# Moving the feed-forward part, the normalised rows and the next rows' flip within the two-layer steps of an interleaved attention and feed-forward kernel

## The chip, the cores and the metric

The kernel runs on one core of a Trainium2 chip. The metric is the device time of one execution in microseconds (us). Three runs of the kernel before the change took 1553.95, 1558.8 and 1562.65 us; their median is 1558.8 us.

The engines of a core work in parallel, each in the order of its own instructions: TensorE (PE in the profile; its weight loads are PEld), VectorE (DVE), ScalarE (ACT), GpSimd (POOL) and SyncE (SP, which here only issues DMAs). They wait for each other through semaphores. TensorE writes to PSUM, which has eight banks.

## The reference

Two layers, each of a recurrent attention part A and a gated feed-forward part B, over 2048 rows of 448 columns:

```
x = x + A(layernorm(x));  x = x + B(layernorm(x))     # layer 1
x = x + A(layernorm(x));  return x + B(layernorm(x))  # layer 2, the same weights

A: for each of 64 segments of 32 rows:
     h = [mem (8 rows), segment (32 rows)]
     q, k, v = h Wq, h Wk, h Wv        # 16 heads of 256
     o = softmax(mask(q k^T / 16)) v, through Wo
     mem = o[:8];  output o[8:]
B: ((max(x Wg, 0)) * (x Wu)) Wd        # 448 -> 1792 -> 448
```

A segment needs the memory that the segment before it leaves, so A is a chain of 64 steps in each layer.

## The kernel before, in words

**Chains and steps.** Layer 1 and layer 2 run as two chains, the second four segments (`LAG`) behind the first. Step `g` does segment `g` of the first chain and segment `g - 4` of the second in the same matmuls, 2 x 40 moving columns. There are 68 steps; `active(g)` says which chains are live, and `two` is true where both are. Every second step (odd `g` from 3 on) also carries the feed-forward part (`Feed`, called `ff`) of 128 rows: 64 of layer 1 and 64 of layer 2. These are the long steps; 30 of them have both chains, and the change touches these alone ("two-layer long steps").

**Before the steps** the weights are folded: `A_sb` holds Wq Wk^T by heads, `B_sb` Wv Wo. So a step has these matmuls:

- `project` (L714): 28 tiles of h with `A_sb` into PSUM tiles `prj`, in banks of six or four tiles (the order is `BANKS`). Half 0 is heads 0 to 7, half 1 the rest. `copies` takes each bank to `TQ` or `TZ`, on DVE or ACT. Of the four chunks of 128 columns, the last holds 64 columns only; `project_early` (L699) does that chunk for four banks ahead of the others, as the first thing of a step, and holds their banks.
- `scores` (L840): `Sm` against the memory and `Sx` against the segment's own rows, each with a softmax on DVE and ACT whose parts (`m0`, `m1`, `x0`, `x1`, index 0 to 3) the step calls one by one.
- `weigh_m`, `weigh_x`: probabilities times h (`ya`, `yb`, `y1`, `y2`), copied to `YB` (Y in the profile). `weigh_x` of a step runs at the start of the next.
- `project_out` (L932): `YB` times `B_sb` into `ox`, 28 tiles (`NT`) of three matmuls for each half; `project_last` (L940) does the last 64 columns into `o3` (o in the profile).
- `finish`: `ox` to the next step's memory columns in `hT` and to `OT`, the rows that A leaves, transposed.

**The feed-forward part of a long step:**

- `residual` (L556): four transposes of `OT` (`otp`), the sum with the rows `xa` on DVE, then `row_stats`: two statistics on DVE and two operations on POOL that make 1/sqrt(variance).
- `norm` (L583): the normalised rows `xn`, on DVE. `fetch` (L586) writes `xn` to DRAM (`dxn`) and reads it back transposed into `xT`, two DMAs issued by SP, the second when the first has landed.
- `open_rows` (L595): opens six PSUM banks (`ups`, `gps`) with the 64-column chunk; it is the first reader of `xT`. `products` and `gated` do the rest, `down` (L652) multiplies with Wd into `dps`, adds and takes statistics; `norm2` (L672) normalises layer 1's rows for layer 2 (`xn` again).
- `feed_on` (L678): four transposes of that `xn` (`tps`) and two copies into the next steps' `hT`: one on DVE, one on ACT.

**What sets the order.** TensorE's order is that of the code: `in_order` ties every matmul to the one before it. `InOrder` does the same for DVE, ACT and SP. Which PSUM bank a tile gets is chosen while the program is built: `bank` (L130) keeps an estimate of when each bank is free, counted in estimated ns of matmul time, and takes the earliest that nothing holds; `after` is the estimated time from the last matmul to the end of the copies. A wrong estimate makes no wrong result: the matmul waits for the copy.

Of the kernel before, what the change touches and what calls it, by code (L numbers as in the profile page):

```python
# [9 lines left out]
F32 = mybir.dt.float32  # L10
# [18 lines left out]
BLK = 2  # L29
TB = BLK * SEG  # L30
NT = 28
# [10 lines left out]
BANKS = (((0, 6), (6, 6), (24, 4), (12, 6), (18, 6)), ((0, 6), (24, 4), (6, 6), (12, 6), (18, 6)))  # L42
# [8 lines left out]
def a_tile(t):  # L51

    if t >= 24:
        return t
    u = t // 12 * 6 + t % 6
    return 3 * (t // 6 % 2 * 4 + u % 4) + u // 4
# [7 lines left out]
def build_kernel(ctx, tc, A_x, A_mem0, A_Wq, A_Wk, A_Wv, A_Wo, B_W_gate, B_W_up, B_W_down, out,  # L64
                 ntiles=16, nseg=64):
    nc = tc.nc
    P = nc.NUM_PARTITIONS
# [62 lines left out]
    def bank(shape, dtype, name, after=700, hold=False):  # L130

        i = min((i for i in range(8) if i not in held), key=lambda i: free_at[i])
        t = psum.tile(shape, dtype, tag=f"b{i}", name=name)
        bank_of[t.name] = (i, after)
        free_at[i] = now[0] + 1000
        if hold:
            held.add(i)
        return t
# [39 lines left out]
    pre = prepare.enter_context(tc.tile_pool(name="pre", bufs=6))  # L178
# [69 lines left out]
    def next_piece():  # L248

        if pieces:  # L250
            spread(sp.dma_start(*pieces.pop(0)))

    hTb = []
# [61 lines left out]
    with prepare:  # L315
# [130 lines left out]
        for p in range(NP):  # L446
            hf, p4 = divmod(p, 4)
# [37 lines left out]
        for p in range(NP):  # L485
            hf, p4 = divmod(p, 4)
# [205 lines left out]
    def tile_of(ps, hf, t, i, chains, hb, j, kds, first, last):  # L692

        n = L * len(chains)
        for kd in kds:
            mm(ps[:, i * n:(i + 1) * n], A_sb[:, kd, hf, a_tile(t), :], moving(hb, j, kd, chains),
               start=first and kd == kds[0], stop=last and kd == kds[-1], skip_group_check=True)

    def project_early(hf, chains, hb, j, pairs=(0, 1), head=0):  # L699

        n = L * len(chains)
        pre = {}
        for pair in [EARLY[i] for i in pairs]:
            for i0 in pair:
                pre[i0] = bank([P, 512], F32, "prj", hold=True)
            for i in range(head):
                tile_of(pre[pair[0]], hf, pair[0] + i, i, chains, hb, j, range(3), i == 0, False)
            for i in range(6):
                for i0, rows in zip(pair, (slice(0, 64), slice(64, 128))):
                    mm(pre[i0][:, i * n:(i + 1) * n], A_sb[rows, 3, hf, a_tile(i0 + i), :], moving(hb, j, 3, chains, rows),  # L710
                       start=(i == 0 and (head == 0 or i0 != pair[0])), stop=False, skip_group_check=True)
        return pre

    def project(hf, chains, hb, j, banks, pre={}, busy=False, first=None, inside=None, head=0):  # L714

        n = L * len(chains)
        for i0, k in banks:
            ps = pre[i0] if i0 in pre else bank([P, 512], F32, "prj")
            two = len(chains) == 2

            def copies(eng, rows, T):
                if two:
                    evac(eng, T, ps[rows, 0:k * n].rearrange("p (t g q) -> p t g q", t=k, q=16))
                    return
                c = chains[0]
                src = ps[rows, 0:k * n].rearrange("p (t w) -> p t w", t=k)
                x, m = (0, SEG) if c == 0 else (MEM, 0)
                evac(eng, T[:, :, 2, MEM * c:MEM * c + MEM], src[:, :, m:m + MEM])
                evac(eng, T[:, :, 3 * c:3 * c + 2, :],
                     src[:, :, x:x + SEG].rearrange("p t (g q) -> p t g q", q=16))  # L730

            for i in range(k):
                if inside is not None and i == 4:
                    inside()
                if i0 not in pre:
                    tile_of(ps, hf, i0 + i, i, chains, hb, j, range(4), True, True)
                elif i >= head or i0 != banks[0][0]:
                    tile_of(ps, hf, i0 + i, i, chains, hb, j, range(3), False, True)
            if i0 in pre:
                let_go(ps)  # L740
            if first is not None:
                first()
            if i0 < 24:
                u0, eo = i0 // 12 * 6, i0 // 6 % 2
                T = TQ[hf][:].rearrange("p g u w -> p g (u w)").rearrange("p g (t e q) -> p t e g q", e=2, q=16)
                T = T[:, u0:u0 + 6, eo]
                copies(act if (i0 != 6 if busy and hf else i0 % 12) else dve, slice(0, P), T)
            else:
                for eng, e in ((act if busy else dve, 0), (act, 1)):
                    copies(eng, FR[e], TZ[hf][FR[e]].rearrange("p g (t e q) -> p t e g q", e=2, q=16)[:, :, e])  # L750
            if i0 in (6, 18):
                next_piece()
# [58 lines left out]
    def step(g, ff, pre, late):  # L811
        chains = active(g)
        xs = active(g - 1)
        ms = [c for c in chains if g - c * LAG + 1 < nseg]
        gb, j = divmod(g, BLK)
        hb = hTb[gb % 2]
# [115 lines left out]
        def project_out(hf, t0, t1):  # L932

            for t in range(t0, t1):
                for mc in range(3):
                    mm(ox[:, mc, lo:hi], B_sb[:, hf, t, mc * 128:(mc + 1) * 128],
                       YB[hf][:, t, lo:hi], start=(hf == 0 and t == 0 and mc == 0),
                       stop=(hf == 1 and t == NT - 1 and mc == 2), skip_group_check=True)
# [39 lines left out]
                    ff.gate_up(u)  # L978


        project(0, chains, hb, j, BANKS[0][0:2], pre)
        hk = hk_make()
        if ff is not None:
            ff.residual()
        next_piece()
        project(0, chains, hb, j, BANKS[0][2:5], pre, ff is not None)
        two = len(chains) == 2
        if ff is not None:
            ff.norm()
            if two:  # L990
# [11 lines left out]
        between = len(chains) == len(xs) == 1  # L1002
# [56 lines left out]
        if ff is not None:  # L1059
            x1[3]()  # L1060
            if len(chains) == 1:
                x0[0]()
                x1[0]()
            ox_open()
            project_out(0, 0, 10)
            ff.open_rows((0, 1, 2))
            if len(chains) == 2:
                x0[0]()
            x0[1]()
            m1[2]()  # L1070
            x0[2]()
            if two:
                px0 = fetched(PX[0], "x0")
            feed(0)
            next_piece()
            if len(chains) == 2:
                x1[0]()
            ff.products(1)
            ff.gated(1)
            pm = flipped(PM[1], 1, "m1", act) if ms else None  # L1080
            x1[1]()
            ff.products(2)
            x1[2]()
            if two:
                px1 = fetched(PX[1], "x1")
            else:
                px0 = flipped(PX[0], 2, "x0", act)
            weigh_m(1, hk, pm)
            ff.gated(2)
            feed(3)  # L1090
            project_out(0, 10, 18)
            next_piece()
            ff.down()
            ff.norm2()
            project_out(0, 18, NT)
            project_last()
            next_piece()
            project_out(1, 0, 12)
            if not two:
                px1 = flipped(PX[1], 2, "x1")  # L1100
            project_out(1, 12, 18)
            ff.feed_on()
            project_out(1, 18, NT)
        else:
            next_piece()
            ox_open()
            m1[2]()
            x0[0]()
            x0[1]()
            late_flip = 23  # L1110
            project_out(0, 0, late_flip)
            pm = flipped(PM[1], 1, "m1") if ms else None
            project_out(0, late_flip, NT)
            weigh_m(1, hk, pm)
            x0[2]()
            x1[3]()
            x1[0]()
            x1[1]()
            x1[2]()
            if two:  # L1120
                px1 = fetched(PX[1], "x1")
            next_piece()
            project_last()
            project_out(1, 0, 10)
            px0 = flipped(PX[0], 2, "x0", act)
            project_out(1, 10, 25)
            if not two:
                px1 = flipped(PX[1], 2, "x1", act)
            next_piece()
            project_out(1, 25, NT)  # L1130
        finish()
        nxt = active(g + 1)
        pre = project_early(0, nxt, hTb[(g + 1) // BLK % 2], (g + 1) % BLK) if nxt else {}
        weigh_x(0, hk, px0)
        return pre, lambda between: weigh_x(1, hk, px1, between)

# [3 lines left out]
    pre, late = project_early(0, active(0), hTb[0], 0), None  # L1140
    for g in range(nsteps):
# [6 lines left out]
        if g % 2 and 0 <= i < nblk + LAG // BLK - 1:  # L1148
            fed = Feed(i)
            pre, late = step(g, fed, pre, late)  # L1150
        else:
            pre, late = step(g, None, pre, late)

    ff = Feed(nblk + LAG // BLK - 1)
# [81 lines left out]
```

## Time and profile before

| | us |
|---|---|
| median of three runs | 1558.8 (1553.95 to 1562.65) |
| the profiled execution | 1555.26 |
| its span, first to last instruction | 1553.5 |
| granted TensorE clock | 1.0 of full speed |
| TensorE matmuls (PE), busy | 1532.4 |
| VectorE (DVE), busy | 1088.7 |
| ScalarE (ACT), busy | 743.3 |
| GpSimd (POOL), busy | 77.5 |

The first 72 us load and fold the weights (the first prj matmul is at 72.1); the steps fill the rest. One prj or ox matmul of 128x80 lasts 202 ns, but they are pipelined: one starts every 36 ns. A busy matmul row is thus not a price; the distance from start to start is.

How to read the lines that follow. A line of the timeline has the start (us from the span's start), the length, the engine, the kernel's line, the operation, what it writes and reads, the shape and how many equal instructions are merged in it; in brackets the idle time of the engine before it and what ended it. Nearly all instructions have the line of a helper (L106, L153, L161), so the names of the tiles tell them apart. A line of the waits has who waited, for whom, and then the sum in us, how often, and the longest. SPq marks a DMA at its issue on SP's queue.

### The profile page before, as it was taken

The page shows a single profiled execution, that of the slowest core. Times are in us where ns is not written, and L with a number is a line of the kernel's source. Part 1 is how long each engine was busy: PE and PEld are TensorE (multiplying, and loading weights), DVE is VectorE, ACT ScalarE, POOL GpSimd, SP SyncE. Part 2 cuts the span into 40 slices and gives each one's busy share as a digit, 9 for nine tenths or more (in the row PEclk, how much of TensorE's full clock was granted, in tenths as well). Part 3 has the DMA queues.
Part 4 walks back from the last instruction along what each step waited for, and adds up shares of the span by engine and source line. Part 5 has one row for each costly group of instructions (what it writes and reads, how often), then busy time and mean ns, then how long its engine had stood idle before and what let it go on. Part 6 is the DMA issues. An engine that isn't in the chain of part 4 may idle for free.

```text
span 1553.5 us, 89067 instructions
## 1 busy us (share of the span) xinstructions
PE 1532.4 (99%) x40635; PEld 1423.2 (92%) x40635; DVE 1088.7 (70%) x3591; ACT 743.3 (48%) x2059; POOL 77.5 (5%) x173
## 2 busy tenths in 40 slices
PE   9999999999999999999999999999999999999998
PEld 6689999999999999999999999999999999989997
DVE  7766676777667677777677777766777776667765
ACT  6754454454444444544444445444444454445444
POOL 3200000000000000000000000000000000000000
PEclk9999999999999999999999999999999999999999
DMA  8620011000010110000011100000111010000100
GB/s 237 214 70 11 20 27 26 25 20 22 23 22 24 27 26 22 24 22 23 22 25 27 26 22 23 22 21 23 25 27 27 20 22 24 20 22 24 23 7 10
DMA packets 88394, 52.23 MB, mean 34 GB/s; under 512 B 48008, under 2 KB 87120, under 8 KB 88016
## 3 DMA queue, kind: packets, MB, share of 16 engines
q1 hardware_dynamic: 85888, 42.33, 10.4%
q8 instruction: 318, 5.21, 1.4%
q0 software_dynamic: 1088, 3.68, 0.7%
q10 hardware_dynamic: 1040, 0.52, 0.1%
q14 instruction: 60, 0.49, 0.1%
HBM read 23.18 MB, written 11.60 MB: 22 GB/s over the span
## 4 chain that ended last, share of the span: by engine, by line
PE 91%; DMA 5%; DVE 2%; POOL 1%; issue 0%; ACT 0%; SPq 0%; DVEq 0%; POOLq 0%
PE prj L153 28%; PE ox L153 25%; PE gps L153 6%; PE ups L153 6%; PE dps L153 6%; PE o L153 5%; PE y L153 4%; PE Sx L153 3%; DMA xT<-dxn 2%; DMA dxn<-xn 2%; PE bps L153 1%; PE Sm L153 1%; PE ya L153 1%; PE yb L153 1%; PE kps L153 1%; PE tpw L161 1%
## 5 line engine op out<-in xcount | busy, mean ns | idle before, releaser
L153 PE MATMUL prj<-hT,A_sb 128*128 128x80 bf16 (+3 forms) x15232 | 545.2, 199 | 0.4 <-ACT hT L106 0.3
L153 PEld LDWEIGHTS <-A_sb 128*128 128x128 bf16 (+1 forms) x15232 | 502.4, 99 | 20.4 <-issue 0.6
L153 PEld LDWEIGHTS <-B_sb 128*128 128x128 bf16 (+1 forms) x15008 | 484.6, 103 | 15.1 <-issue 2.1
L153 PE MATMUL ox<-Y,B_sb 128*128 128x80 bf16 (+2 forms) x11256 | 436.1, 200 | 1.8 <-issue 1.8
L106 ACT CAST TQ<-prj 128x480 bf16<-128x480 f32 (+1 forms) x380 | 184.2, 497 | 94.6 <-PE prj L153 78.4
L106 ACT CAST Y<-y 128x512 bf16<-128x512 f32 (+2 forms) x392 | 136.9, 419 | 101.6 <-PE y L153 95.8
L106 DVE CAST Y<-y 128x256 bf16<-128x256 f32 x376 | 151.2, 458 | 39.2 <-PE y L153 38.9
L106 ACT ACTIVATE se<-se 128x160 f32<-128x160 f32 (+2 forms) x270 | 81.6, 302 | 189.5 <-DVE se L106 184.9
L106 DVE CAST TQ<-prj 128x480 bf16<-128x480 f32 (+1 forms) x228 | 128.7, 573 | 7.6 <-PE prj L153 7.0
L153 PE MATMUL gps<-xT,Wg_sb 128*128 128x128 bf16 (+3 forms) x1904 | 128.7, 215 | 0.0
L153 PE MATMUL ups<-xT,Wu_sb 128*128 128x128 bf16 (+3 forms) x1632 | 107.0, 215 | 9.6 <-DMA xT<-dxn 9.2
L153 PEld LDWEIGHTS <-Wg_sb 128*128 128x128 bf16 (+1 forms) x1904 | 106.8, 97 | 9.5 <-issue 9.4
L153 PEld LDWEIGHTS <-Wu_sb 128*128 128x128 bf16 (+1 forms) x1904 | 105.7, 97 | 5.6 <-issue 0.2
L106 DVE SCALAR_TENSOR_TENSOR hh<-gps,ut 128x512 bf16<-128x512 f32 (+2 forms) x136 | 78.1, 595 | 43.7 <-PE gps L153 20.5
L106 ACT COPY os<-o 64x16 f32<-64x16 f32 (+3 forms) x134 | 25.6, 191 | 171.9 <-PE o L153 170.3
L153 PEld LDWEIGHTS <-hk 40*128 40x128 bf16 (+1 forms) x1950 | 98.8, 96 | 7.9 <-DMA PT<-dx 0.5
L106 DVE TENSOR_REDUCE ssum<-se 128x4 f32<-128x160 f32 (+2 forms) x270 | 73.4, 272 | 42.3 <-ACT se L106 38.5
L106 ACT CAST TZ<-prj 64x320 bf16<-64x320 f32 (+2 forms) x264 | 96.9, 377 | 8.2 <-DVE TZ L106 5.3
L153 PE MATMUL dps<-Wd_sb,hh 128*128 128x448 bf16 (+1 forms) x504 | 93.3, 342 | 0.8 <-DVE hh L106 0.8
L106 ACT CAST ut<-ups 128x512 bf16<-128x512 f32 (+1 forms) x102 | 57.4, 563 | 64.0 <-PE ups L153 64.0
L106 DVE CAST Y<-ya 128x256 bf16<-128x256 f32 x134 | 56.9, 425 | 43.8 <-PE ya L153 43.3
L153 PEld LDWEIGHTS <-TQ 128*128 128x128 bf16 x1938 | 85.7, 96 | 1.3 <-ACT TQ L106 0.9
(138 smaller groups left out, 1800.7 us busy)
## 6 DMA issues: line engine op xcount, KB each, us to landing
dx<-PX SPq DMA_DIRECT2D x90, 64.0 KB, 1.6
dxn<-xn SPq DMA_DIRECT2D x29, 128.0 KB, 1.7
wo<-in_A_Wo_dram POOLq DMA_DIRECT2D x8, 448.0 KB, 5.1
nat<-in_A_Wv_dram SPq DMA_DIRECT2D x8, 384.0 KB, 4.9
nat<-in_A_Wq_dram SPq DMA_DIRECT2D x6, 384.0 KB, 5.1
nat<-in_A_Wk_dram SPq DMA_DIRECT2D x6, 384.0 KB, 5.0
xa<-in_A_x_dram SPq DMA_DIRECT2D x32, 56.0 KB, 2.8
xa<-xp SPq DMA_DIRECT2D x32, 56.0 KB, 1.9
```

The costliest lines, as they stand in the source:

```text
L106: r = f(*a, **k)
L153: in_order(nc.tensor.matmul(out, lhsT, rhs, **k))
L161: in_order(nc.tensor.transpose(out, src, idn))
```

## The change

Only two-layer long steps (`two` and `ff`) get another order, and with the order the planner's choice of banks changes in all steps.

- `residual` is called inside `project`, after the matmuls of the first bank and ahead of that bank's copy. It stood after the second bank and `hk_make` (`kps`). On DVE the sum and the two statistics now stand ahead of the first `TQ` copy.
- The planner gets 2200 ns and not 700 as the time to free that first bank, for the steps where this holds.
- `open_rows` follows 18 tiles of `project_out` of half 0, not 10. The next eight tiles still stand between the last products and `down`; two, not ten, are left for after `norm2`.
- `feed_on` stands behind tile 20 and not tile 18 of half 1.

```diff
-    def project_early(hf, chains, hb, j, pairs=(0, 1), head=0):
+    def project_early(hf, chains, hb, j, pairs=(0, 1), head=0, after=700):
...
-                pre[i0] = bank([P, 512], F32, "prj", hold=True)
+                pre[i0] = bank([P, 512], F32, "prj", 700 if i0 else after, hold=True)
...
-    def project(hf, chains, hb, j, banks, pre={}, busy=False, first=None, inside=None, head=0):
+    def project(hf, chains, hb, j, banks, pre={}, busy=False, first=None, inside=None, head=0, between=None):
...
             if first is not None:
                 first()
+            if between is not None:
+                between()
...
-        project(0, chains, hb, j, BANKS[0][0:2], pre)
+        two = len(chains) == 2
+        early = ff is not None and two
+        project(0, chains, hb, j, BANKS[0][0:1], pre, between=ff.residual if early else None)
+        project(0, chains, hb, j, BANKS[0][1:2], pre)
         hk = hk_make()
-        if ff is not None:
+        if ff is not None and not two:
             ff.residual()
...
-            project_out(0, 0, 10)
+            mid = 18 if two else 10
+            project_out(0, 0, mid)
             ff.open_rows((0, 1, 2))
...
-            project_out(0, 10, 18)
+            project_out(0, mid, mid + 8)
             next_piece()
             ff.down()
             ff.norm2()
-            project_out(0, 18, NT)
+            project_out(0, mid + 8, NT)
             project_last()
...
-            project_out(1, 12, 18)
+            fed = 20 if two else 18
+            project_out(1, 12, fed)
             ff.feed_on()
-            project_out(1, 18, NT)
+            project_out(1, fed, NT)
...
-        pre = project_early(0, nxt, hTb[(g + 1) // BLK % 2], (g + 1) % BLK) if nxt else {}
+        after = 2200 if len(nxt) == 2 and g % 2 == 0 else 700
+        pre = project_early(0, nxt, hTb[(g + 1) // BLK % 2], (g + 1) % BLK, after=after) if nxt else {}
```

## The prediction

> **What bounds the kernel.** I read the engine shares first, then the chain of work that ended last, then TensorE's waits, then the rows of one long step.
>
> ```profile
> PE 1532.4 (99%) x40635; PEld 1423.2 (92%) x40635; DVE 1088.7 (70%) x3591; ACT 743.3 (48%) x2059; POOL 77.5 (5%) x173
> PE 91%; DMA 5%; DVE 2%; POOL 1%; issue 0%; ACT 0%; SPq 0%; DVEq 0%; POOLq 0%
> ```
>
> TensorE (PE) is busy for the whole span, and the chain leaves it only for DMA. So a change that adds no matmul can win only what PE waits for. TensorE's waits name it:
>
> ```profile
> PE ups L153 <- DMA xT<-dxn: 9.2, 10, 2.2
> PE ox L153 <- issue: 1.8, 3, 1.3
> PE dps L153 <- DVE hh L106: 0.8, 1, 0.8
> PE y L153 <- DMA PT<-dx: 0.3, 1, 0.3
> PE prj L153 <- ACT hT L106: 0.3, 1, 0.3
> ```
>
> The first feed-forward matmul (ups) waits for the flipped, normalised rows xT. The timeline around the longest of these waits shows the chain behind it (rows of PE, DVE, POOL and SP):
>
> ```profile
> 1356.02 0.39 PE L161 MATMUL otp<-ident,OT 128*128 128x128 bf16 x4
> 1356.45 0.39 DVE L106 TENSOR_TENSOR xa<-otp,xa 128x448 bf16<-128x448 bf16 x1 [0.27 <-PE otp L161]
> 1356.87 0.63 DVE L106 BATCH_NORM_STATS2 stats<-xa 128x6 f32<-128x448 bf16 x1
> ...
> 1357.66 0.66 DVE L106 CAST TQ<-prj 128x480 bf16<-128x480 f32 x1
> ...
> 1358.11 0.57 POOL L278 TENSOR_TENSOR rstd<-rstd,half 128x1 f32<-128x1 f32 x1
> 1358.71 0.61 DVE L106 TENSOR_SCALAR xn<-xa,mv,rstd 128x448 bf16<-128x448 bf16 x2 [0.39 <-POOL rstd L278]
> ...
> 1359.34 0.33 SPq L106 DMA_DIRECT2D dxn<-xn  x1
> ...
> 1362.87 1.20 SPq L106 DMA_TRANSPOSE xT<-dxn  x1
> ...
> 1367.18 0.21 PE L153 MATMUL ups<-xT,Wu_sb 64*128 64x128 bf16 x1 [2.21 <-DMA xT<-dxn]
> ```
>
> Read step by step in the same way, all 30 long steps with two layers have 3.13 us from the first otp transpose to the end of xn; only the two DMAs vary. The copy dxn lands 1.65 to 3.5 us after its issue (median 1.67), the flip xT 2.4 to 4.3 us after its own. Without a wait the first ups starts 5.56 us after dxn's issue and 0.134 us after the matmul before it; a late one starts 0.04 us after xT's landing. The starts are late in 11 steps, by 1.75, 1.92, 0.47, 1.44, 0.24, 0.27, 0.25, 0.07, 0.25, 1.07 and 2.27 us: 10.0 us (the waits' 9.2 leave out gaps under 0.15). In the steps that are on time two steps take 44.27 us, always.
>
> **The change, part by part.** I place times in the long step whose otp starts at 644.86.
>
> *Feed-forward behind 18 tiles.* Eight tiles of three ox matmuls move ahead of the first ups: 24 x 36 ns (start to start in ox rows) = 0.86 us more for xT. The sum of matmuls is the same, and eight tiles still stand between the last products and the down projection. The orders on VectorE (DVE) and ScalarE (ACT) do not change here; PX1's softmax, behind the first product hh on DVE, comes up to 0.86 us later, and so does its fetch, which SP issues at 661.95 (2.4 us to landing) for a reader at 673.67.
>
> *Rows flipped sooner.* The four otp transposes jump over 18 prj matmuls (0.65 us) and four kps (0.21 us): they run at 644.01, 0.85 us sooner. They need OT, whose last copy ends at 642.98, and their bank, whose last reader (ACT, Y) ends at 643.83. DVE ends its Y copies at 644.45, and then takes xa (0.39), the statistics (0.63 + 0.18) and only then the TQ copy (0.65) that used to stand first. POOL's rstd is ready at about 646.7. But xn also stands behind the second TQ copy, which waits for its matmuls and still ends at 647.16 as before. So xn starts at 647.14 and not 647.54: **0.41 us** sooner, not 0.85. No DMA is added; dxn and xT keep their order on SP's queue, which has nothing else in those microseconds. The first TQ copy ends at 646.3 and not 645.0: its first reader runs at 648.67, and its PSUM bank is next written by a y matmul after 647.5, because the planner now holds that bank for 2200 ns; without that cover each 0.1 us late would cost 3 us in 30 steps. kps is 0.22 us later; ACT has 0.43 us idle before its next TQ copy.
>
> *The next rows' flip two tiles back.* This is where the change can lose. The end of the long step, from the timeline:
>
> ```profile
> 667.47 0.39 PE L161 MATMUL tps<-ident,xn 128*128 128x128 bf16 x4
> 667.70 1.24 PE L153 MATMUL ox<-Y,B_sb 128*128 128x80 bf16 x30
> 667.90 0.29 DVE L106 COPY hT<-tps 128x256 bf16<-128x256 bf16 x1 [0.80 <-PE tps L161]
> 668.22 0.37 ACT L106 COPY hT<-tps 128x256 bf16<-128x256 bf16 x1 [2.16 <-DVE hT L106]
> 668.87 0.60 PE L153 MATMUL prj<-hT,A_sb 64*128 64x80 bf16 x24
> ```
>
> ACT's copy waits for DVE's, and the next step's first prj for ACT's. From the first tps to ACT's end are 1.12 us; PE comes 0.05 us after that (the one such wait: ACT ends at 135.80, PE starts at 135.85). PE's way is now 24 matmuls and not 30: 1.40 - 0.215 = 1.185 us against 1.17: 15 ns to spare. Upstream, the ox matmuls between the down projection and the last columns (o) shrink from 30 to 6, those between o and the flip grow from 54 to 60: the down projection ends 0.86 us nearer to the step's end, and so does its chain on DVE (sum, statistics, sum, xn): xn ends at 667.40 against a tps that starts at 667.68; the sums behind xn (hT, OT) end at 667.96 and the hT copy can start at 668.11. Spare: about 0.2 and 0.12 us. I cost this at nothing with 0.4 us in all for jitter around 15 ns (30 x 0.015). From both sides: a release of 0.03 us (DVE to ACT, above) gives no wait; one of 0.09 us (DVE to POOL, 646.55 to 646.64) makes 0.025 x 30 = 0.8 us. The value lies nearest to the PE row, so 0.4.
>
> *Sum.* Each late start shrinks by 0.86 + 0.41 = 1.27 us or to nothing: 0.48 + 0.65 + 0.17 + 1.00 = 2.3 us are left of 10.0; the gain is 7.7 us. If a DMA issued sooner did not land sooner, only 0.86 counts: 4.15 us are left, and the gain is 5.9 us. Nothing in these rows ties a landing to the clock time, so I take 7.7. The profiled execution took 1555.3 us (span 1553.5): 1555.3 - 7.7 + 0.4 = **1548.0 us**. The median of the runs is 1558.8, 3.5 us above it. Runs differ by 8.7 us, as much as these waits amount to; if they are what differs, each run falls to about the same floor (1555.3 - 10.0 = 1545.3 plus 1 to 3 us), and 1548 holds for the median too. If something else differs, the median falls to 1551.
>
> [...]
>
> **The rivals.**
>
> *DMAs that keep to their fast times.* If the late landings were an accident of this execution, and dxn took 1.67 and xT 2.6 us throughout, the sum of 4.3 stays below 5.56, no start is late, and before and after both take 1545.3. Against it: 12 of 30 steps exceed 5.4 us, spread over the whole span, and the three runs lie 8.6 us or more above 1545.3. Chance 0.03; no difference between the kernels. [...]
>
> *The landing doesn't come sooner, or the runs differ by something else.* Then 5.9 us from 1558.8: 1553. For it: I know no cause of the late landings. Chance 0.16.
>
> *A bank comes free too late.* All PSUM banks are dealt anew. What speaks against it: the otp bank has 0.13 us of cover, the y bank over 1 us. A late bank of 0.2 us a step costs 6 us: 1554. Chance 0.10.
>
> *The flip comes too late (the slower side).* DVE works in order, and the hT copy stands behind xn and three sums. Should that queue run late by one more operation of its kind (the xa sum of 0.62 us), the copy starts 0.5 us late, eats the 0.015 us, and PE waits 0.485 us in each of 30 steps: 14.6 us against a gain of 7.7, so 1555.3 + 6.9 = 1562.2; up to 1567 at 0.8 us. It decides from 0.38 us of lateness on DVE (0.12 spare, then 0.26 a step eats the gain). Against it: DVE sits idle 0.80 us before that copy now. Chance 0.09.
>
> **How the numbers follow.** Forecast: chance 0.62, 1548.0, its own range 1544.5 to 1551.5. A measurement of this kernel can tell about 0.5% from no change, which is 7.8 us: below 1551.0 is faster. Of the forecast 0.57 lie there and 0.05 above. The rivals at 1553, 1554 and no difference add 0.29 to "same"; the slower one splits 0.03 and 0.06. Faster 0.57, same 0.37, slower 0.06. The range 1544 to 1556 holds the forecast and the rivals at 1553 and 1554 and leaves out the slow one.
>
> **What would show it.** Right: ups's wait for xT falls from 9.2 us to about 2 in at most 4 or 5 steps; xn no longer waits 0.39 us for POOL in long steps; xn ends about 3.6 us, not 3.13, after the first otp starts (0.85 sooner start, 0.41 sooner end); on-time pairs of steps still take 44.27 us. Wrong: a wait of prj for ACT's hT in every long step, a pair of steps longer than 44.3 us, a new wait of y, otp or prj for a copy, or xT's landings that move later by what the issue moved sooner.

## The result, and the profile after

After the change the kernel takes **1552.25 us** (median of 8 runs, 1546.99 to 1557.06); the kernel before took 1561.6 (8 runs, 1553.95 to 1568.59, its first three among them). The ratio is 0.9939, 95% interval 0.9913 to 0.9966. The profiled execution took 1552.72 us, its span 1550.9. The forecast was 1548.0 and faster. The kernel is faster, by 0.6%, and the interval leaves out 1; its time is 4.3 us above the forecast and within its range.

The page's busy line and the shares of the chain that ended last, after:

```profile
PE 1533.7 (99%) x40635; PEld 1423.9 (92%) x40635; DVE 1092.4 (70%) x3591; ACT 744.3 (48%) x2059; POOL 77.6 (5%) x173
PE 96%; DMA 2%; DVE 1%; issue 0%; ACT 0%; POOL 0%; SPq 0%; DVEq 0%; ACTq 0%; POOLq 0%
```

No matmul was added, and the DMA share of the chain fell from 5% to 2%. TensorE's waits after (who waits, for whom; sum in us, how often, longest):

```profile
PE y L153 <- DMA PT<-dx: 4.1, 3, 2.2
PE ox L153 <- issue: 1.7, 3, 1.0
PE ups L153 <- DMA xT<-dxn: 1.2, 2, 0.7
PE dps L153 <- DVE hh L106: 0.8, 1, 0.8
```

The wait of ups for xT is nearly gone: 1.2 us where it was 9.2. But a wait that had been 0.3 us now leads: y for PT. That is layer 2's `weigh_x` in a long step. Its PT comes by two DMAs (dx, PT) whose code stands in the short step ahead, and the change touched none of it.

The way of xT in the later of the two late steps (timeline, step 21 of the 30):

```profile
1042.07 0.39 PE L161 MATMUL otp<-ident,OT 128*128 128x128 bf16 x4
...
1044.17 0.57 POOL L278 TENSOR_TENSOR rstd<-rstd,half 128x1 f32<-128x1 f32 x1
1044.56 0.66 DVE L106 CAST TQ<-prj 128x480 bf16<-128x480 f32 x1 [0.25 <-PE prj L153]
1045.13 0.60 DVE L106 TENSOR_SCALAR xn<-xa,mv,rstd 128x448 bf16<-128x448 bf16 x2
...
1049.08 1.20 SPq L106 DMA_TRANSPOSE xT<-dxn  x1
...
1053.20 0.21 PE L153 MATMUL ups<-xT,Wu_sb 64*128 64x128 bf16 x1 [0.47 <-DMA xT<-dxn]
```

POOL's rstd ends 0.39 us ahead of xn, and xn starts right behind the second TQ copy: no wait for POOL is shown at it. Even so dxn took 3.3 us and xT 4.1. Of these 7.4, 6.9 lie under other work; 5.56 did before.

The end of a long step after, where the flip has to be in time:

```profile
663.30 0.39 PE L161 MATMUL tps<-ident,xn 128*128 128x128 bf16 x4
...
663.73 0.29 DVE L106 COPY hT<-tps 128x256 bf16<-128x256 bf16 x1 [0.15 <-PE tps L161]
664.05 0.37 ACT L106 COPY hT<-tps 128x256 bf16<-128x256 bf16 x1 [2.38 <-DVE hT L106]
664.48 0.60 PE L153 MATMUL prj<-hT,A_sb 64*128 64x80 bf16 x24
```

DVE's idle time ahead of the hT copy is 0.15 us (it was 0.80), and ACT's copy ends 0.06 us ahead of prj (it was 0.27). PE starts that prj 0.134 us after the ox matmul before it in all 30 steps, as before: no wait.

The two spans differ by 2.6 us only. Waits of 8.7 us for xT went (10.0 to 1.3, counted from start to start), and 4.5 us for PT came (0.5 to 5.0). After the longest of these TensorE's granted clock also fell. The wait, and the busy time of each engine from 733.70 to 737.00, where the column behind POOL's is the clock:

```profile
733.89 0.61 PE L153 MATMUL y<-PT,hk 40*128 40x256 bf16 x10 [2.19 <-DMA PT<-dx]
```

```profile
733.70:737.00 3.30, 3.11 (x56) 2.96 (x57) 1.70 (x5) 1.70 (x5) 0.00 (x0) 0.61 0.17 40
```

The records show one stretch of 3.41 us at half speed here, 1.7 us lost. So 10.5 us of waits before (10.0 + 0.5) stand against 8.0 us after (1.3 + 5.0 + 1.7).

### The profile page after: what moved, and what is told of

It is laid out like the page before. It is cut to its first block, busy times and chain, and to the rows that moved or that the text cites. A ratio compares the mean times of both kernels' runs of the same rounds, so it can differ in the third digit from the quotient of the medians.

```text
span 1550.9 us, 89067 instructions
## 1 busy us (share of the span) xinstructions
PE 1533.7 (99%) x40635; PEld 1423.9 (92%) x40635; DVE 1092.4 (70%) x3591; ACT 744.3 (48%) x2059; POOL 77.6 (5%) x173
## 3 DMA queue, kind: packets, MB, share of 16 engines
q8 instruction: 318, 5.21, 1.4%
## 4 chain that ended last, share of the span: by engine, by line
PE 96%; DMA 2%; DVE 1%; issue 0%; ACT 0%; POOL 0%; SPq 0%; DVEq 0%; ACTq 0%; POOLq 0%
PE prj L153 31%; PE ox L153 25%; PE gps L153 6%; PE ups L153 6%; PE dps L153 6%; PE o L153 5%; PE y L153 4%; PE Sx L153 3%; PE bps L153 1%; PE Sm L153 1%; PE ya L153 1%; PE aps L153 1%; PE yb L153 1%; PE tpw L161 1%; PE kps L153 1%; PE pps L161 1%
## 5 line engine op out<-in xcount | busy, mean ns | idle before, releaser
L153 PE MATMUL prj<-hT,A_sb 128*128 128x80 bf16 (+3 forms) x15232 | 551.8, 199 | 1.0 <-issue 0.6
L153 PE MATMUL y<-PT,hk 40*128 40x256 bf16 (+1 forms) x1280 | 86.0, 248 | 4.3 <-DMA PT<-dx 4.1
```

The source lines that it names most:

```text
L153: in_order(nc.tensor.matmul(out, lhsT, rhs, **k))
```

## The experiments

The theory: TensorE pays for late landings alone, and the change wins by more cover for xT. Cover is the time from the issue of the first DMA on the way (dxn for xT) to the first matmul that reads the result, when that matmul does not have to wait. The rivals: the gain comes from the order or the banks; and, once the PT waits were seen, the change brings those about.

**One half each.** `e1_tiles` keeps the 18 tiles and the later flip, without the rows sooner; `e2_rows` keeps only the rows sooner.

Their edits, against after:

```diff
-        early = ff is not None and two
+        early = False
...
-        if ff is not None and not two:
+        if ff is not None and not early:
             ff.residual()
...
-        after = 2200 if len(nxt) == 2 and g % 2 == 0 else 700
+        after = 700
```

```diff
-            mid = 18 if two else 10
+            mid = 10
...
-            fed = 20 if two else 18
+            fed = 18
```

> The change without its second part: feed-forward behind 18 tiles and the flip two tiles back, but the otp transposes stay behind the second bank and kps, and the planner's 2200 is 700 again. Theory (cover): TensorE loses only what late landings leave uncovered; from the issue of dxn to the first ups there are 5.56 + 0.86 = 6.42 us. Laid on the landings of the two profiles, waits of ups for xT come to 2.7 to 4.1 us in 4 or 5 steps, against 7.6 to 10.0 at the old cover; on-time pairs of steps stay at 44.27 us; ratio to the kernel before about 0.9965. Rival (order): the gain comes from the new order on VectorE or from other PSUM banks, not from cover; then this kernel, which keeps the old order on VectorE, gains nothing: ratio 1.0.

> The second part alone: otp transposes, sum and statistics sooner with the planner's 2200, feed-forward behind 10 tiles and flip behind tile 18 as before. Theory (cover): 0.41 us more, 5.97 us in all; waits of ups for xT 4.6 to 6.4 us in 5 or 6 steps, pairs of steps at 44.27 us, ratio about 0.998. Rival (order): the whole gain is here, ratio 0.994 and pairs of steps under 44.27 us.

Measured, against before at 1564.98 on that chip: `e1_tiles` 1558.29, ratio 0.9945 (0.9923 to 0.9967); `e2_rows` 1556.28, ratio 0.9947 (0.9921 to 0.9973). Both gain more than expected, each alone about what the whole change gained (0.9939); the three intervals overlap, so the times do not divide the gain between the halves. The cover from dxn's issue to the first ups is 5.56 before, 6.42 in `e1_tiles`, 6.04 in `e2_rows` and 6.90 after: it adds up exactly, 0.86 + 0.48. The waits do not: ups waits 5.1 us in 4 steps in the first (2.7 to 4.1 expected) and 2.1 in 4 in the second (4.6 to 6.4 expected), which has less cover. The landings of the first would have cost 11.1 us under the old cover, those of the second 5.55: which steps land late, and by how much, depends on more than the cover. Steps without a late landing take 44.27 us a pair in both, as before and after, so the new order and the other banks win nothing by themselves. The second half's ratio is nearer to its rival (0.994) than to the theory (0.998); why it gained so much is taken up with the landings below.

**The flip two tiles further back** (tile 22), to have the price of the side on which the change could lose.

```diff
-            fed = 20 if two else 18
+            fed = 22 if two else 18
```

> The changed kernel with the flip two tiles further back, behind tile 22. In the profile after, ACT's hT copy ends 0.057 us ahead of the next step's first prj, and a prj that waits starts 0.05 us after such a copy: under 0.01 us is spare. Theory (the spare is used up at 20): six matmuls of 36 ns less, so each long step waits 0.21 us, 6.2 us in all; pairs of steps take 44.48 us and the time is 6 us above the changed kernel's (ratio to the kernel before about 0.998). Rival (the switch from 128-row to 64-row matmuls, 0.134 instead of 0.036 us, overlaps with more of the wait): under 0.1 us a step, 3 us or less.

The end of a long step in `e3_flip22`:

```profile
667.12 0.81 PE L153 MATMUL ox<-Y,B_sb 128*128 128x80 bf16 x18
...
667.65 0.37 ACT L106 COPY hT<-tps 128x256 bf16<-128x256 bf16 x1 [2.59 <-DVE hT L106]
...
668.07 0.61 PE L153 MATMUL prj<-hT,A_sb 64*128 64x80 bf16 x24
```

prj now follows ACT's end (668.02) by 0.05 us, and the last ox start by 0.342 us, not 0.134: 0.208 us in each of 30 steps, nearly all of the 0.215 us that 6 matmuls of 36 ns take. But the matmuls of prj and y right behind it take 0.04 us less than in after, so a pair on time takes 44.44 us and not the 44.48 expected: the price is 0.17 us a step, 5 us in all, and not 6.2. The time is 1557.74 us, the ratio to before 0.9948 (0.9927 to 0.9969), where about 0.998 was expected; after was not run beside it on that chip, so the 5 us are read from the trace and not from the times. The margin at tile 20 is real and no wider than one tile.

**The kernel before and after again.** One more execution of after with its times, two of before.

> The kernel before, unchanged, for a second profile. The profile before shows 10.0 us of late xT and only 0.5 us of late PT at y, while four of the five profiles taken since, with the same 5.9 us of cover for PX1's fetch, show 4.9 to 7.7 us of the latter. Theory (both fetches draw from the same late landings; the first profile was lucky at y): 7 to 11 us of waits for xT, 4 to 8 us for PT at y, possibly one or two stretches of half clock of 1.7 us each behind idle times over 2 us; span 1556 to 1563. Rival (the change and its parts brought the y waits): y waits under 1 us again, span 1551 to 1555.

> The kernel before, unchanged but for a comment, for a third profile: as for the second. Theory: 4 to 8 us of waits of y for PT; rival: under 1 us.

> The changed kernel, unchanged, timed beside the kernel before once more and profiled a second time. Theory (cover): waits of ups for xT 0 to 2.5 us, of y for PT 4 to 8 us, pairs of steps at 44.27 us; ratio 0.993 to 0.996. Rival (the two parts' gains add, since each part alone measured 0.9945 to 0.9947): ratio 0.989.

`after_2` took 1554.02 us against 1567.68, ratio 0.9912 (0.9881 to 0.9942). That lies between the theory (0.993 to 0.996) and the rival that the halves' gains add (0.989), and the interval reaches both: it does not decide. PT was late by 1.3 us only, not by the 4 to 8 expected. TensorE's waits in the slower execution of before:

```profile
PE ups L153 <- DMA xT<-dxn: 10.3, 6, 2.3
PE y L153 <- DMA PT<-dx: 5.7, 4, 2.1
```

So the PT waits are not the change's: before has them too, and its first profile was a lucky one. In us, by how late TensorE started; the half clock by its stretches of 3.41 us from the first step on, of which half is lost:

| | span | xT late | PT late | half clock |
|---|---|---|---|---|
| before | 1553.5 | 10.0 | 0.5 | 0 |
| before_2 | 1561.7 | 13.3 | 4.1 | 1 x 1.7 |
| before_3 | 1568.5 | 11.0 | 6.8 | 5 x 1.7 |
| after | 1550.9 | 1.3 | 5.0 | 1 x 1.7 |
| after_2 | 1547.7 | 1.4 | 1.3 | 0 |

The xT of `before_2` was late by more than the 7 to 11 us expected. What is left of the span is 1542 to 1545 us in all five. The gain of the change is in the column of xT, 10 us, perhaps with some of the last, where one execution alone stands out.

**PT sooner.** In short steps with both chains, PX1's softmax and fetch go ahead of PX0's, whose own flip moves from tile 10 to tile 22: `e4_px1` on top of after, `e5_px1_before` on top of before.

```diff
-            x0[0]()
-            x0[1]()
+            ahead, behind = (x1, x0) if two else (x0, x1)
+            if two:
+                x1[3]()
+            ahead[0]()
+            ahead[1]()
...
             weigh_m(1, hk, pm)
-            x0[2]()
-            x1[3]()
-            x1[0]()
-            x1[1]()
-            x1[2]()
+            ahead[2]()
             if two:
                 px1 = fetched(PX[1], "x1")
+            else:
+                x1[3]()
+            behind[0]()
+            behind[1]()
+            behind[2]()
...
-            project_out(1, 0, 10)
+            turn = 22 if two else 10
+            project_out(1, 0, turn)
             px0 = flipped(PX[0], 2, "x0", act)
-            project_out(1, 10, 25)
+            project_out(1, turn, 25)
```

> The changed kernel, and in the two-chain steps without feed-forward the softmax of PX1 runs ahead of that of PX0, so that PX1's fetch is issued about 2.2 us sooner; PX0's flip on TensorE moves from tile 10 to tile 22. Theory (what is left of the waits is mostly the same kind of late landing on PX1's fetch, read by y in the long step, where 5.9 us of cover stand against landings of up to 8.2 us): the waits of y for PT (4.1 us in the profile after) go to 0 to 0.2 us; the time falls to the floor of 1545 plus 1 to 2 us of xT waits, 1546 to 1547 (ratio about 0.9905 to the kernel before). Rival (those waits were an accident of one profile): time as the changed kernel, ratio 0.994. Second rival: PX0's flip behind tile 22 is late and weigh_x waits in each step.

> The kernel before with PX1's softmax and fetch sooner in the two-chain steps without feed-forward, as in the run e4_px1, and nothing of the change. Theory (PX1's fetch is late in the kernel before as well): waits of y for PT fall to 0.2 us or less, waits for xT stay at 7 to 11 us, and the time falls by the usual 4 to 8 us of y waits: ratio 0.995 to 0.997. Rival (late PX1 fetches belong to the changed kernel alone): ratio 0.9995 or more.

`e4_px1` takes **1548.24 us** (6 runs), ratio to before 0.9887 (0.986 to 0.9913); 1546 to 1547 was expected; its span is 1544.6, y waits nowhere in the two-layer steps, and TensorE's clock stays whole. It beats the kernel before; after was not run beside it on that chip (`g3_after_half` and `g4_px1_half` below make that comparison). `e5_px1_before` takes 1561.91, ratio 0.9959 (0.9937 to 0.9982): no wait of y again, xT still late by 7.75 us, with one stretch at half clock. The two repairs are separate. TensorE's wait for xT in `e4_px1`, where PT no longer shows:

```profile
PE ups L153 <- DMA xT<-dxn: 0.8, 2, 0.5
```

**Why landings are late.** Over the profiles of before and after, dxn is late in the same steps again and again: 1, 4, 5, 9, 13, 17, 20, 21, 24, 25 and 28 in three executions of before, but for two differences. The DMA view shows beside such a landing a packet of the queue "instruction". There are 318 of these on q8, of 16,384 B each: 5.21 MB. TensorE's instructions are 81,270 in the profile (40,635 matmuls, as many weight loads): 64.1 B for each, one packet for 255.6 of them. From this count come the estimates that q8 carries TensorE's instructions and that one packet has 256 of them, and a run can break them: 64 small matmuls on zeros ahead of the first step (128 instructions with the weight loads) shift the packets by half (`g1_half`), 128 by a whole one (`g2_whole`).

```diff
         keep_warm(3)
+        junk = bank([P, 512], F32, "junk")
+        for _ in range(64):
+            in_order(nc.tensor.matmul(junk[:, 0:8], still[:, 0:128], still[:, 0:8], start=True, stop=True))
```

> The kernel before, with 64 small matmuls on zeros (128x8, their results are never read) ahead of the first step; nothing else moves. The steps are numbered 1 to 30 (two-layer long steps). In three profiles of the kernel before, dxn lands late (over 2.0 us after its issue) in nearly the same steps: 1, 4, 5, 9, 13, 17, 20, 21, 24, 25 and 28. Theory, instruction fetch: TensorE's instructions come in packets of 16 KB, one for each 256 of them (a matmul is two, with its weight load), and dxn is late only where such a packet begins between 0.5 us ahead of its issue and 1.2 us behind it, xT where one begins 0.5 to 2.2 us behind its issue. 64 matmuls are 128 instructions, half a packet: every packet comes 64 matmuls sooner within its step, some 2.4 us. By the packets of the kernel before, moved by so much, steps 3, 7, 11, 15 and 19 are late, with 22 or 23, 26 and 30, and steps 5, 9, 13, 17 and 21 land in 1.7 us. Rival, place: the late landings belong to the place of a step in the program or to its data, and the same eleven steps are late as before. Rival, chance: another set without a rule, not the one named.

> The same with 128 small matmuls: 256 instructions, one whole packet. Theory, instruction fetch: the packets fall where they fell in the kernel before, so the same steps are late: at least nine of 1, 4, 5, 9, 13, 17, 20, 21, 24, 25 and 28, and 3, 7, 11, 15 and 19 land in 1.7 us. Rival, place: the same set here and with 64 matmuls. Rival, chance or clock time (the steps begin at another time by some us): a set that is unlike that of the kernel before in both runs.

In `g1_half` dxn is late in 3, 4, 7, 11, 15, 18, 19, 22, 23, 25, 26, 27 and 30: all that the theory named are there, four that it did not name (4, 18, 25 and 27) too, and 5, 9, 13, 17 and 21 land in 1.7 us. In `g2_whole` it is late in all eleven of the old steps, and in 16 and 29; 3, 7, 11, 15 and 19 land in 1.7. Step 5 in the DMA view, from 0.5 us ahead of dxn's issue to 1.2 behind it (queue, packets, MB, share; then the issue with its us to landing), in before, `g1_half` and `g2_whole`:

```profile
q8 instruction: 1, 0.02, 4.6%
issues: line engine op xcount, KB each, median us to landing
dxn<-xn SPq DMA_DIRECT2D x1, 128.0 KB, 3.1
```

```profile
q1 hardware_dynamic: 121, 0.12, 19.7%
issues: line engine op xcount, KB each, median us to landing
dxn<-xn SPq DMA_DIRECT2D x1, 128.0 KB, 1.7
```

```profile
q8 instruction: 1, 0.02, 4.9%
issues: line engine op xcount, KB each, median us to landing
dxn<-xn SPq DMA_DIRECT2D x1, 128.0 KB, 3.1
```

The packet is there, gone, and there again, and the landing goes with it; in step 7 it is the other way round (1.7, 2.9, 1.7). Behind the added matmuls the same steps, data and DMAs stand in all three, so the rival "place" falls, and chance with it. Both runs took as long as before (one run each: 1572.24 and 1568.27 against 1568.38): another set of steps, not a smaller one.

A late dxn keeps to the packet and not to its own issue: 129 late landings of all profiles have a q8 packet in that stretch, and they come 2.4 us after the packet begins (median; nine in ten between 2.1 and 2.9), whether it begins ahead of the issue or up to 1.2 us behind it. So the place of dxn's issue among the packets counts too. Steps 4, 9, 20 and 24 are late in all five profiles with the old issue (three of before, `e1_tiles`, `e5_px1_before`) and in none of the five with the sooner one (two of after, `e2_rows`, `e3_flip22`, `e4_px1`); step 29 is the other way round. Under the old cover the landings of the first five would have cost 7.7 to 13.3 us, of the others 5.6 to 8.7. So a part of what the sooner rows won seems to be the place and not the cover. Why this place is the better one is open; it is so too with the packets shifted by half (14.9 us in `g1_half`, 9.0 and 11.0 in `g3_after_half` and `g4_px1_half` below).

**Does the gain hang on where the packets fall?** The same 64 matmuls on top of after and of `e4_px1`.

> The kernel after, with the 64 small matmuls ahead of the first step: half an instruction packet. Theory, instruction fetch: another set of steps is late than in the two profiles of the kernel after (there dxn is late in 1, 13, 17, 21, 25 and 29 in both; by their packets, moved by 64 matmuls, those but perhaps 21 land in 1.7 us and the late ones are others), but about as many, so ups waits 0.5 to 3 us for xT, y 2 to 7 us for PT, and the time is 1549 to 1556. Rival, luck: the gain of the change hangs on where the packets fell; then ups waits 6 us or more again and the time is that of the kernel before.

> The same 64 matmuls in the fastest kernel so far (PX1's softmax and fetch ahead of PX0's in the short steps, PX0's flip from tile 10 to 22). Theory: its fetch of PT has cover enough for any place of the packets, so y waits under 0.3 us, ups 0.5 to 4 us for xT, TensorE keeps its clock but for at most one stretch, and the time is 1546 to 1551, 2 to 6 us below the kernel after on the same chip. Rival, luck: y waits 1 to 5 us again and the two kernels take the same time.

`g3_after_half` takes 1554.24 us, ratio to before 0.9941 (0.9914 to 0.9969); dxn is late in nine other steps than after, none of 1, 13, 17, 21, 25 and 29; ups waits 3.1 us for xT, y 7.6 for PT, with three stretches at half clock (its profiled run is its slowest, 1564.38). The xT wait is thus 0.1 us, the PT wait 0.6 us above what was expected. `g4_px1_half` takes 1549.05 us, ratio 0.9919 (0.9891 to 0.9948): no wait of y, ups 2.2 us for xT, no half clock in the steps. It lies 5.2 us below `g3_after_half` on that chip, and its time has the 64 matmuls in it. So both gains are there at both places of the packets that were tried.

## Why the prediction was right, and where not

- *The bound, and what the cover buys.* Right in the sum: ups waits 1.3 us in 2 steps (2.3 in 4 expected), and the landings of after would have cost 7.6 us under the old cover of 5.56. Not right step by step: shrinking each late start by 1.27 us leaves steps 1, 5, 9 and 28 late, but late are 1 and 21 in the first profile of after, 5 and 21 in the second.
- *0.86 us from the tiles, 0.41 from the rows.* 0.86 and 0.48. xn stands behind the second TQ copy, as said; "3.13" and "about 3.6" were measured from the last of the four otp, and the second came out at 3.49 in every step. (Of the 30 steps before, 14 and not 12 have DMAs of over 5.4 us.)
- *Flip on the edge, 15 ns to spare.* Right, and priced by `e3_flip22`: at tile 20 ACT ends 57 ns ahead of prj, and a prj that waits starts 50 ns after ACT. The flip there costs nothing, not 0.4 us.
- *Banks.* Right: no wait of 0.2 us in every step, pairs on time at 44.27 us.
- *"The landing doesn't come sooner."* This rival is half true. A dxn that met no packet landed 1.7 us after its issue (median 1.68 over all 14 profiles, 6 of 232 above 2.0), so there a sooner issue is a sooner landing; a late one landed by the packet (2.4 us after it began, median). It would have left 4.15 us of xT waits, and 1.3 and 1.4 were left.
- *Fast DMAs throughout.* Fell: dxn alone took 1.67 to 3.64 us after, xT 2.41 to 5.01.
- *"Each run falls to about the same floor (1545.3 plus 1 to 3 us), and 1548 holds for the median too."* This step failed, by 4.3 us. It took xT for all that differs between runs; 1551, which the prediction gave for the other case, is nearer to 1552.25. The profile of before showed 0.3 us for PT, and the step read it as a property of the kernel; `before_2` and `before_3` show 4.1 and 6.8, and clock losses up to 8.5. After keeps the PT wait (5.0, 1.3) and some of the clock. `e4_px1`, which takes the PT wait away, comes to 1548.24.
- *The gain.* 7.7 less 0.4 forecast for the profiled execution; 9.4 (medians) and 13.7 measured. The missing part is probably that execution's luck: xT was late by 10.0 us in it, by 11.0 and 13.3 in the two others, and half clock took 8.5 and 1.7 us more of these. By the prediction's own line, faster is below 1551.0, which 1552.25 is not; but that line was drawn from a kernel before at 1558.8, and beside after it took 1561.6.
- *"Nothing in these rows ties a landing to the clock time"* was true of the rows shown and wrong of the trace: the instruction packets were in the DMA view of the same window.

## What to carry to other kernels

A wait for a DMA that shows as 0.3 us in one profile (y for PT in `before`) was 5.7 us in another of the same kernel (`before_3`): before a floor is forecast, compare the cover of every DMA with the slowest landing of its kind, not with its own wait in that run. Here 5.9 us of cover for PT stood against a slowest dx of 3.5 and a slowest PT of 4.2 us in the very first trace, where they never fell together; after, they did (3.8 + 4.4). The order that moved the fetch sooner cost no matmul (40,635 before and after); the flip moved towards its reader was free while its copy ended 0.057 us ahead of the reader, and two tiles more cost 0.17 us in every step (`e3_flip22`).

## What the runs showed of the hardware

*dxn and xT land late beside instruction packets.* Over all 14 profiles, where no instruction packet begins between 0.5 us ahead of dxn's issue and 1.2 behind it, 226 of 232 landings take at most 2.0 us (median 1.68); where one does, 140 of 188 take longer (median 2.44, up to 3.9). For xT the time is 0.45 to 2.25 us behind the issue: 168 of 195 over 3.0 us with a packet, 30 of 225 without. Both instruction queues are counted here, q8 and, with packets of up to 8,192 B, q14; by q8 alone 129 of 143 dxn are late with a packet and 17 of 277 without. The bounds were read from three of the profiles, before the shifted runs. How the packet holds the others up was not tried. In the two-layer steps TensorE was late for the copies that it waits for, and itself shows no gap of over 0.5 us without a releaser. In the one-layer steps at both ends of the program there are such gaps: 41 in 14 profiles, all at 79 to 126 or 1514 to 1526 us, and each ends 1.2 to 1.6 us after a q8 packet has ended (in before a gap of 1.45 us, at 84.36, 1.34 us after one). That TensorE waits there for its instructions is the author's estimate, and no run tested it.

*The clock fell beside some late starts, of 1.45 to 2.61 us.* In the two-layer steps of 14 profiles the clock fell to half 18 times, for 3.41 us each, and each time between 0.2 us ahead of a late TensorE start and 1.5 us behind it. That start was late, counted from the one before, by 1.86 to 2.61 us. 15 other gaps of 1.8 us or more, up to 2.57, were not followed by it, and no shorter one there was. But in the first step, at 83 to 88 us, the clock fell four times more, and the gaps beside these were of 1.45, 1.72, 1.72 and 2.07 us: the length of a gap alone does not tell which are followed. What decides which gaps are followed stays open.
